# Two attentions on one core: local attention's channels loaded in quarters of 32 partitions, and a split made in place

## The chip, the cores and the metric

The kernel runs on one core of a Trainium2 chip. The metric is the device time of one execution in microseconds (us); the median of three runs is given. The core's engines run side by side: TensorE (PE for its matmuls, PEld for its weight loads), VectorE (DVE), ScalarE (ACT), GpSimd (POOL), and SyncE (SP), which here does nothing but issue DMAs. Each engine works through its own instructions in order and waits for semaphores.

## The reference, cut to what matters

```python
S, D, H, Dh, W, dil = 2048, 576, 32, 18, 8, 2
# A: local, dilated: each position sees itself and 7 positions 2, 4, ... 14 before it
q, k, v = heads(A_x @ A_wqkv)
idx = pos[:, None] - dil * arange(W)          # masked where negative
logits = einsum("bhsd,bhswd->bhsw", q, k[idx]) * Dh ** -0.5
a = merge(einsum("bhsw,bhswd->bhsd", softmax(logits), v[idx])) @ A_wo
# B: full attention of the same size
q, k, v = heads(B_x @ B_wqkv)
b = merge(softmax(q @ k.T * Dh ** -0.5) @ v) @ B_wo
return concatenate([a, b], -1)                # 1 x 2048 x 1152, float32
```

## The kernel before, in words

Matmuls take their operands as a rounded high part and a remainder, so most inputs are split in two on the way: ACT copies the high part (a copy that rounds), POOL or DVE subtracts it from the raw value.

*First phase, to about 422 us: the projections of A and B.* `inputs` (L387) splits the rows of x chunk by chunk. A is 576 = 4 x 128 + 64 rows deep; the last 64 rows of x are loaded twice into one tile of 128 partitions, so that their high part and their remainder lie in the two halves of one tile, `xhl` (L401): ACT copies the high part into one half (L404), copies the other half's high part into a helper tile `ohi` (L405), and POOL or DVE writes the other half's remainder from raw and helper (L406). The name `ohi` is a ring of four buffers. It is shared: the copies of projection results on their way to DRAM take from it too (L462 with its store at L468 into `dqk`, and L651 with its store at L652 into `da`). The transposed projections of A lie in DRAM as `da`, 3 x 576 rows (the channels of q, k, v) of 14 + 2048 positions; the 14 are the halo before the first position.

*Second phase, 422 to 1635 us: 512 steps* (`while step < ALL`, L1132). They are the 8 groups of 4 heads, 4 blocks of 512 queries each, 16 tiles of 128 keys each of B's full attention. A step makes four score matmuls (L229) with ACT's exponentials (L235), three or four matmuls whose results DVE reduces to the maxima that a later block needs (L159, L166), and the weighted sums of an earlier tile (L701). Sixteen steps are one block. After each block `finish` (L706) divides by the row sums: at one step after the block's end SP loads the 2048 sums into `den` (L733), at eight DVE takes the reciprocals (L734), at nine SP stores them, at thirteen SP loads them spread out as `rec` (L736), and at eighteen POOL multiplies (L737). Other things on SP are the `place` loads of maxima (L192, eight of 2 KB for a block), the stacks of later groups (L144), outputs, and the loads of A.

*A's local attention* is POOL's work beside the steps. It is cut into eight sub-blocks of 256 positions (`local(j)`, L815). A sub-block lies on 128 partitions: 4 quarters of 64 positions times 32 heads, with 18 channels x 64 positions (q) or 18 x 78 (k and v, with their halo) along each partition. The products with q and k are L841 to L848, those with v L884 to L887. Sub-block j has its origin at step 10 + 54 j.

What sets the order is written out by hand: each function appends pieces to `agenda` at a step, `due()` runs those of the current step, and each engine's instructions stand in the order in which they were issued so. A SP load therefore waits behind all SP loads issued before it. SP's DMAs use eight semaphores in turn, so each also waits until the one issued eight before it has landed.

Before the change a sub-block's data come in two hops. `arrange(n)` (L820), for n = q, k, v, copies from `da` to a DRAM tensor `dpart`, which holds the sub-block in the tile's order (4 quarters x 576 channels x 64 or 78 positions): one DMA each of 576, 702 and 702 KB, in runs of 256 or 312 bytes. The three are issued at consecutive steps, 24 steps ahead of the origin or at the fourteenth step of that block if that is later (j = 4: steps 206 to 208). `fetch(nm)` (L826) then loads `dpart` into the tile in one DMA over 128 partitions: q at the origin, k one step later, v 28 steps later. The tile of q has one buffer, k and v share two.

Of the kernel before, what the change touches and what calls it, by code (L numbers as in the profile page):

```python
# [7 lines left out]
F32 = mybir.dt.float32  # L8
F32R = mybir.dt.float32r
BF16 = mybir.dt.bfloat16  # L10
AF = mybir.ActivationFunctionType
# [5 lines left out]
S = 2048  # L17
D = 576
H = 32
DH = 18  # L20
# [9 lines left out]
NJ = S // AB  # L30
SUB = AB // 4
HALO = DIL * (W - 1)

STEPS = NB * NT
# [9 lines left out]
GAP = 54  # L44

A_FROM = 10


def ap(t, *dims):

    return bass.AP(tensor=t.tensor, offset=t.offset, ap=[list(t.ap[0])] + [list(d) for d in dims])


def rows(t, *dims):

    return bass.AP(tensor=t.tensor, offset=t.offset, ap=[list(d) for d in dims])
# [3 lines left out]
def two_attentions(ctx: ExitStack, tc, xa, wa, woa, xb, wb, wob, out):  # L60
# [5 lines left out]
    nc = tc.nc  # L66
    load = nc.sync.dma_start

    const = ctx.enter_context(tc.tile_pool(name="const", bufs=1))
    dram = ctx.enter_context(tc.tile_pool(name="dram", bufs=1, space=DRAM))  # L70
# [9 lines left out]
    def bank(kind=None):  # L80
# [6 lines left out]
    dqk = dram.tile([2, 2 * D, S], F32, name="dqk")  # L87
    dv = dram.tile([NG, 128, NT, 4 * 19], F32, name="dv")


    da = dram.tile([3 * D, HALO + S], F32, name="da")
    dparts = [[dram.tile([4, D, (HALO if n else 0) + SUB], F32, name=f"dpart{n}{j}") for n in range(3)]
              for j in range(NJ)]
    dao = dram.tile([NJ, 2, 4, D, SUB], F32, name="dao")
    drec = dram.tile([NG, NB, 4, 512], F32, name="drec")
    do = dram.tile([2, NG - 1, 128, S], F32, name="do")
# [242 lines left out]
    with (tc.tile_pool(name="x", bufs=1, side="right") as xp,  # L339
# [14 lines left out]
        def staged(src, cols, dims, into, spare=False):  # L354

            n = sum(m for _, m in cols)
            wide = src.shape[1]
            raws = {}

            def get(c, issue=load):  # L360
                t = raws[c] = raw(spare)
                for at, r0, m in [(0, 128 * c, 128)] if c < 4 else [(0, 512, 64), (64, 512, 64)]:
                    issue(ap(t[at : at + m], (n // len(cols), len(cols)), (1, n // len(cols))),  # L363
                          rows(src[r0, cols[0][0]], (wide, m), *dims))

            return get, lambda c: into(c, raws[c][:, :n])

        def split(engine, hi, lo, t):
            nc.scalar.activation(hi, t, AF.Copy)  # L369
            engine.tensor_sub(lo, t, hi)  # L370
# [19 lines left out]
        def inputs(src, b, engine, spare=False):  # L390
            x = [[], [], None]

            def into(c, t):
                if c < 4:
                    hi, lo = (xp.tile([128, 512], F32R, name=nm, bufs=4 * NB) for nm in ("xhi", "xlo"))
                    x[0].append(hi)
                    x[1].append(lo)
                    split(engine, hi, lo, t)
                else:

                    hl = x[2] = xp.tile([128, 512], F32R, name="xhl", bufs=NB)  # L401
                    high = xp.tile([128, 512], F32R, name="ohi", bufs=4)
                    one, other = (slice(64 * (b % 2), 64 * (b % 2) + 64), slice(64 - 64 * (b % 2), 128 - 64 * (b % 2)))
                    nc.scalar.activation(hl[one], t[one], AF.Copy)  # L404
                    nc.scalar.activation(high[other], t[other], AF.Copy)  # L405
                    engine.tensor_sub(hl[other], t[other], high[other])  # L406

            return x, *staged(src, [(512 * b, 512)], [(512, 1), (1, 512)], into, spare)

# [30 lines left out]
        qkv, odd = ExitStack(), ExitStack()  # L440
# [3 lines left out]
        if True:  # L444
# [34 lines left out]
            for c in range(5):  # L479
                one, other = (load, nc.scalar.dma_start) if c % 2 == 0 else (nc.scalar.dma_start, load)  # L480
# [159 lines left out]
            for k in range(2, 14):  # L640
                n = 46 if k == 2 else 36 + 4 * k
# [7 lines left out]
            def leave_a(c, b, n, ps):  # L649
                o = xp.tile([128, 512], F32, name="ohi", bufs=4)  # L650
                nc.scalar.activation(o[:n], ps, AF.Copy)  # L651
                load(da[128 * c : 128 * c + n, HALO + 512 * b : HALO + 512 * b + 512], o[:n])  # L652
# [23 lines left out]
            for c, b in order:  # L676
                n = min(128, 3 * D - 128 * c)
                work_list.append(((b % 2, ws[c][0], xas[b][0], slice(0, n), every),
                                  lambda ps, n=n: ps[:n], lambda ps, c=c, b=b, n=n: leave_a(c, b, n, ps)))
# [16 lines left out]
    work = ctx.enter_context(tc.tile_pool(name="work", bufs=1, reuse_waits="tile"))  # L696
# [118 lines left out]
    def local(j):  # L815

        st = {}
        p0 = AB * j

        def arrange(n):  # L820
            wide = (HALO if n else 0) + SUB
            load(rows(dparts[j][n][0, 0], (wide, D), (D * wide, 4), (1, wide)),
                 rows(da[D * n, HALO + p0 + SUB - wide :], (HALO + S, D), (SUB, 4), (1, wide)))


        def fetch(nm):  # L826
            halo = 0 if nm == "q" else HALO
            n = DH * (halo + SUB)
            t = st[nm] = work.tile([128, DH, halo + SUB], F32, name="akv" if halo else "aq", bufs=2 if halo else 1)
            load(ap(t, (1, n)), rows(dparts[j]["qkv".index(nm)][0, 0], (n, 128), (1, n)))  # L830

        def window(t, c):

# [46 lines left out]
        def weighted(c):  # L880
            if c == 0:
                st["o"] = work.tile([128, DH, SUB], F32, name="ao", bufs=1)
            at = wide()
            nc.gpsimd.tensor_mul(at, ap(st["lg"], (0, 2), (SUB, W), (1, SUB)), window(st["v"], c))  # L884
            nc.gpsimd.tensor_add(at[:, :, :4], at[:, :, :4], at[:, :, 4:])  # L885
            nc.gpsimd.tensor_add(at[:, :, :2], at[:, :, :2], at[:, :, 2:4])
            nc.gpsimd.tensor_add(st["o"][:, 2 * c : 2 * c + 2], at[:, :, 0], at[:, :, 1])  # L887
# [10 lines left out]
        def put(i):  # L898
            load(rows(dao[j, i, 0, 0], (DH * SUB, 128), (1, DH * SUB)),
                 ap(st["parts"][i].bitcast(F32), (1, DH * SUB)))  # L900
# [18 lines left out]
        def sums_of_a(h):  # L919
# [3 lines left out]
            if h == 0:  # L923
# [3 lines left out]
            nc.scalar.activation(y, two, AF.Copy)  # L927
            behind_scores.append(lambda: nc.vector.tensor_add(y, one, y))

        pieces = [(0, lambda: fetch("q")), (1, lambda: fetch("k")), (28, lambda: fetch("v")), (33, lower),  # L930
                  (35, exponents), (39, share), (60, upper), (61, rest), (64, lambda: put(0)), (66, lambda: put(1))]

        pieces[:0] = [(at, lambda f=f, n=n: f(n)) for f, ats in ((most, (31, 32, 33)), (total, (36, 37, 38)),
                                                                (inverses, (38, 39))) for n, at in enumerate(ats)]
        for c in range(DH // 2):
            pieces.append((5 + 5 * c // 2, lambda c=c: match(c)))
            pieces.append((39 + 5 * c // 2, lambda c=c: weighted(c)))
        at = A_FROM + GAP * j - 24

        at = max(at, STEPS * (at // STEPS) + 14) - A_FROM - GAP * j  # L940
        for n in range(3):
            pieces.append((at + n if j else n - 7, lambda n=n: arrange(n)))
        for n, (at, ends) in enumerate(((70, (78, 80)), (81, (87, 89)))):
            pieces.append((at, lambda n=n: get(n)))
            for h in range(2):
# [144 lines left out]
    for j in range(NJ):  # L1090
        plan(A_FROM + GAP * j, local(j))
# [15 lines left out]
    rest = NG * NB * PIECES * 2 - early  # L1107
# [24 lines left out]
    while step < ALL:  # L1132
        n, kt = divmod(step, NT)
# [51 lines left out]
```

## Time and profile before

| what | time |
|---|---|
| median of 3 runs | 1646.02 us (1645.42 to 1647.79) |
| the profiled execution | 1646.54 us |
| its span, first to last instruction | 1644.8 us |
| PE busy | 1633.1 us |
| DVE busy | 1397.0 us |
| ACT busy | 1221.9 us |
| POOL busy | 959.2 us |
| data moved by DMA | 188.22 MB, 114 GB/s on the mean |

The profile gives for each engine the time in which it worked; issuing DMAs is not counted as work, so SP has a queue but no busy share. PE's and PEld's times overlap. A row of a timeline gives the start, the duration, the engine and line, the operation, the tiles (out <- in) and the count; in brackets stands the idle time before it and what ended it. For a DMA on SP's queue the duration is the time that SP's sequencer stood on that instruction, waits included, not the transfer. The chain of work that ended last is followed back from the last instruction: a piece that isn't PE is a place at which PE waited for it. In a table of windows the last three columns are the granted clock of PE as a share of full speed, the share of time in which the 16 DMA engines were busy (packets of several queues overlap, so it can exceed 1), and the data rate.

### The profile page before, as it was taken

What the parts mean: (1) busy time and instruction counts of PE and PEld (TensorE: products, weight loads), DVE (VectorE), ACT (ScalarE), POOL (GpSimd) and SP (SyncE); (2) the same over time, 40 slices, a digit from 0 to 9 for tenths busy, and PEclk for the clock granted to TensorE, in tenths of its full rate; (3) what the DMA queues carried; (4) which work ended last, traced back from release to release, by engine and by line L of the source; (5) the groups of instructions that cost most, each with busy time, mean ns of one, the idle gap of its engine ahead of it and who ended that gap; (6) DMA issues with size and microseconds to landing.
All of it is one profiled execution on the core that took longest, in us unless ns stands there. A gap on an engine that the chain in (4) does not pass through costs nothing.

```text
span 1644.8 us, 33745 instructions
## 1 busy us (share of the span) xinstructions
PE 1633.1 (99%) x12906; PEld 935.0 (57%) x12906; DVE 1397.0 (85%) x2366; ACT 1221.9 (74%) x2419; POOL 959.2 (58%) x792
## 2 busy tenths in 40 slices
PE   9999999999999999999999999999999999999998
PEld 7999879998433444444344344344344344445676
DVE  5199989999899989889889899889899989888533
ACT  6314432111899998998998998998998998998554
POOL 2306642210195995994994994994995996940000
PEclk9999999999999999999999999999999999999999
DMA  8837955522515347157139325716526132033201
GB/s 252 238 113 204 257 165 140 134 87 90 95 48 100 98 120 135 54 139 143 53 93 161 82 77 130 147 65 122 134 79 117 65 107 78 21 114 123 101 37 59
DMA packets 188353, 188.22 MB, mean 114 GB/s; under 512 B 118384, under 2 KB 132208, under 8 KB 186464
## 3 DMA queue, kind: packets, MB, share of 16 engines
q1 hardware_dynamic: 183328, 174.53, 40.9%
q0 software_dynamic: 4032, 10.63, 3.0%
q8 instruction: 101, 1.65, 0.4%
q10 hardware_dynamic: 832, 0.92, 0.2%
q14 instruction: 60, 0.49, 0.1%
HBM read 113.16 MB, written 88.12 MB: 122 GB/s over the span
## 4 chain that ended last, share of the span: by engine, by line
PE 96%; DMA 2%; DVE 1%; ACT 0%; POOL 0%; issue 0%; SPq 0%; ACTq 0%; POOLq 0%; DVEq 0%
PE po L701 30%; PE bank L229 25%; PE bank L322 16%; PE bank L159 13%; PE bank L1010 7%; PE bank L259 5%; DMA den<-o 1%; DVE mx L166 1%; DMA dqk<-ohi 0%; POOL xlo L370 0%; DMA first<-xb 0%; DVE am L859 0%; SPq L363 0%; DMA out<-y 0%; PE bank L985 0%
## 5 line engine op out<-in xcount | busy, mean ns | idle before, releaser
L166 DVE TENSOR_REDUCE mx<-bank 128x1 f32<-128x512 f32 x2048 | 1288.1, 683 | 144.6 <-PE bank L159 115.8
L235 ACT ACTIVATE e<-bank 128x512 f32<-128x512 f32 x2048 | 1060.2, 613 | 94.3 <-PE bank L229 51.0
L159 PE MATMUL bank<-ks,qs 54*128 54x512 f32 x2048 | 752.7, 423 | 2.1 <-DVE mx L166 2.0
L229 PEld LDWEIGHTS bank<-qs,ks 56*128 56x128 f32 x2048 | 331.1, 186 | 454.1 <-ACT e L235 423.6
L229 PE MATMUL bank<-qs,ks 56*128 56x512 f32 x2048 | 582.0, 425 | 0.0
L701 PE MATMUL po<-e,v 128*19 128x512 f32 x4096 | 538.1, 599 | 0.0
L159 PEld LDWEIGHTS bank<-ks,qs 54*128 54x128 f32 x2048 | 340.8, 185 | 15.6 <-DVE mx L166 7.6
L841 POOL TENSOR_TENSOR pr<-aq,akv 128x1024 f32<-128x1024 f32 x72 | 158.4, 2201 | 28.1 <-DMA akv<-dpart 25.6
L701 PEld LDWEIGHTS po<-e,v 128*19 128x19 f32 x4096 | 70.6, 97 | 182.1 <-issue 171.4
L884 POOL TENSOR_TENSOR pr<-lg,akv 128x1024 f32<-128x1024 f32 x72 | 158.1, 2196 | 0.6
L845 POOL TENSOR_TENSOR pr<-pr 128x1024 f32<-128x1024 f32 x64 | 152.5, 2382 | 5.0
L651 ACT ACTIVATE ohi<-bank 128x512 f32<-128x512 f32 (+1 forms) x56 | 30.5, 595 | 148.3 <-issue 116.9
L322 PE MATMUL bank<-xlo,ahi 64*128 64x512 f32 (+1 forms) x448 | 117.9, 389 | 1.4 <-POOL xlo L370 1.4
L322 PE MATMUL bank<-xhi,alo 64*128 64x512 f32 (+1 forms) x448 | 116.1, 388 | 0.0
L322 PE MATMUL bank<-xhi,ahi 64*128 64x512 f32 (+1 forms) x448 | 113.7, 388 | 1.1 <-ACT ohi L651 1.1
L885 POOL TENSOR_TENSOR pr<-pr 128x512 f32<-128x512 f32 x72 | 92.3, 1282 | 5.6
L370 POOL TENSOR_TENSOR alo<-raw,ahi 128x512 fp32r<-128x512 f32 (+1 forms) x14 | 17.6, 1254 | 121.1 <-ACT ahi L369 86.7
L463 POOL TENSOR_TENSOR olo<-olo,ohi 128x512 fp32r<-128x512 f32 x36 | 46.1, 1294 | 63.8 <-ACT ohi L462 58.4
L737 POOL TENSOR_TENSOR o<-o,rec 128x512 f32<-128x512 f32 x29 | 37.2, 1284 | 64.3 <-DMA rec<-drec 35.4
L322 PEld LDWEIGHTS bank<-xlo,ahi 64*128 64x128 f32 (+1 forms) x448 | 67.2, 182 | 7.6 <-POOL xlo L370 2.5
L322 PEld LDWEIGHTS bank<-xhi,alo 64*128 64x128 f32 (+1 forms) x448 | 65.8, 182 | 5.3
L322 PEld LDWEIGHTS bank<-xhi,ahi 64*128 64x128 f32 (+1 forms) x448 | 63.8, 181 | 7.2 <-ACT ohi L651 1.5
(197 smaller groups left out, 1790.5 us busy)
## 6 DMA issues: line engine op xcount, KB each, us to landing
do<-n SPq DMA_DIRECT2D x28, 512.0 KB
da<-ohi SPq DMA_DIRECT2D x52, 256.0 KB
dpart<-da SPq DMA_DIRECT2D x16, 702.0 KB
akv<-dpart SPq DMA_DIRECT2D x16, 702.0 KB
out<-y SPq DMA_DIRECT2D x32, 288.0 KB
qs<-dqk SPq DMA_DIRECT2D x30, 288.0 KB
ks<-dqk SPq DMA_DIRECT2D x30, 288.0 KB
at<-dao SPq DMA_DIRECT2D x64, 128.0 KB
```

The costliest lines, as they stand in the source:

```text
L159: nc.tensor.matmul(ps, qs[at, b, p, 128 * t : 128 * t + 128], ks[at, p, 512 * k : 512 * k + 512], start=True, stop=True)
L166: nc.vector.tensor_reduce(mx[:, r, p, t, k : k + 1], ps, axis=AX.X, op=ALU.max)
L229: nc.tensor.matmul(ps, ks[at, p, 128 * kt : 128 * kt + 128], qs[at, b, p], start=True, stop=True)
L235: nc.scalar.activation(e, ps, AF.Exp, scale=SCALE)
L259: nc.tensor.matmul(ps, a, b, start=c == i == 0, stop=c == 4 and i == 1)
L322: nc.tensor.matmul(ps, a, b, start=start, stop=stop)
L701: nc.tensor.matmul(po[32 * i : 32 * i + 19], vs[g][:, kt, 19 * i : 19 * i + 19], es[i], start=kt == 0, stop=kt == NT - 1)
L841: nc.gpsimd.tensor_mul(pr, ap(st["q"][:, 2 * c], (SUB, 2), (0, W), (1, SUB)), window(st["k"], c))
L845: nc.gpsimd.tensor_add(st["pr"], st["pr"], pr)
L884: nc.gpsimd.tensor_mul(at, ap(st["lg"], (0, 2), (SUB, W), (1, SUB)), window(st["v"], c))
L885: nc.gpsimd.tensor_add(at[:, :, :4], at[:, :, :4], at[:, :, 4:])
L1010: nc.tensor.matmul(ps, a, b, start=start, stop=stop)
```

## The change

The DRAM tensors `dpart` and the function `arrange` are gone. `fetch(nm, s)` loads quarter s of q, k or v, 32 partitions, straight from the rows of `da`: 32 heads x 18 channels x 64 or 78 positions, 576 runs of 256 or 312 bytes, 144 or 175.5 KB. A sub-block has twelve such DMAs where it had three copies and three fetches. For j > 0 the quarters of q are issued at 18, 16, 14 and 12 steps before the origin, those of k at 10, 8, 6 and 4 before it, those of v at 16, 18, 20 and 22 after it; for j = 0 those of q and k at nine to two steps before it, one per step.

In `inputs`, the last rows' high part of the other half is copied straight into `xhl` and the remainder written over it by a subtraction in place. The helper tile from the ring `ohi` is not taken any more.

The instructions of PE, DVE, ACT and POOL are the same in number and in order; only SP's differ.

```diff
-    dparts = [[dram.tile([4, D, (HALO if n else 0) + SUB], F32, name=f"dpart{n}{j}") for n in range(3)]
-              for j in range(NJ)]
...
                     hl = x[2] = xp.tile([128, 512], F32R, name="xhl", bufs=NB)
-                    high = xp.tile([128, 512], F32R, name="ohi", bufs=4)
                     one, other = (slice(64 * (b % 2), 64 * (b % 2) + 64), slice(64 - 64 * (b % 2), 128 - 64 * (b % 2)))
                     nc.scalar.activation(hl[one], t[one], AF.Copy)
-                    nc.scalar.activation(high[other], t[other], AF.Copy)
-                    engine.tensor_sub(hl[other], t[other], high[other])
+                    nc.scalar.activation(hl[other], t[other], AF.Copy)
+                    engine.tensor_sub(hl[other], t[other], hl[other])
...
-        def arrange(n):
-            wide = (HALO if n else 0) + SUB
-            load(rows(dparts[j][n][0, 0], (wide, D), (D * wide, 4), (1, wide)),
-                 rows(da[D * n, HALO + p0 + SUB - wide :], (HALO + S, D), (SUB, 4), (1, wide)))
-
-        def fetch(nm):
+        def fetch(nm, s):
             halo = 0 if nm == "q" else HALO
-            n = DH * (halo + SUB)
-            t = st[nm] = work.tile([128, DH, halo + SUB], F32, name="akv" if halo else "aq", bufs=2 if halo else 1)
-            load(ap(t, (1, n)), rows(dparts[j]["qkv".index(nm)][0, 0], (n, 128), (1, n)))
+            if s == 0:
+                st[nm] = work.tile([128, DH, halo + SUB], F32, name="akv" if halo else "aq", bufs=2 if halo else 1)
+            load(st[nm][32 * s : 32 * s + 32],
+                 rows(da[D * "qkv".index(nm), HALO + p0 + SUB * s - halo :],
+                      (DH * (HALO + S), H), (HALO + S, DH), (1, halo + SUB)))
...
-        pieces = [(0, lambda: fetch("q")), (1, lambda: fetch("k")), (28, lambda: fetch("v")), (33, lower),
-                  (35, exponents), (39, share), (60, upper), (61, rest), (64, lambda: put(0)), (66, lambda: put(1))]
+        pieces = [(33, lower), (35, exponents), (39, share), (60, upper), (61, rest), (64, lambda: put(0)), (66, lambda: put(1))]
...
-        at = A_FROM + GAP * j - 24
-
-        at = max(at, STEPS * (at // STEPS) + 14) - A_FROM - GAP * j
-        for n in range(3):
-            pieces.append((at + n if j else n - 7, lambda n=n: arrange(n)))
+
+        for nm, at, apart in (("q", -18, 2), ("k", -10, 2)) if j else (("q", -9, 1), ("k", -5, 1)):
+            pieces += [(at + apart * i, lambda nm=nm, i=i: fetch(nm, i)) for i in range(4)]
+        pieces += [(16 + 2 * i, lambda i=i: fetch("v", i)) for i in range(4)]
```

## Prediction

> **What bounds the kernel now.** I read the page first (shares, then the chain that ended last), then the chain and the queues around its largest DMA piece, then the one ACT wait on the lines that the change edits.
>
> ```profile
> span 1644.8 us, 33745 instructions
> ...
> PE 1633.1 (99%) x12906; PEld 935.0 (57%) x12906; DVE 1397.0 (85%) x2366; ACT 1221.9 (74%) x2419; POOL 959.2 (58%) x792
> ...
> PE po L701 30%; PE bank L229 25%; PE bank L322 16%; PE bank L159 13%; PE bank L1010 7%; PE bank L259 5%; DMA den<-o 1%; DVE mx L166 1%; DMA dqk<-ohi 0%; POOL xlo L370 0%; DMA first<-xb 0%; DVE am L859 0%; SPq L363 0%; DMA out<-y 0%; PE bank L985 0%
> ```
>
> TensorE is busy for 1633.1 of 1644.8 us, so all that any change of loads can give back is 11.7 us of idle time, and whatever a lowered clock stretches. The change doesn't touch a matmul. It can pay only where the chain leaves PE, and there two entries are DMAs of the middle of the kernel: `den<-o` and `dqk<-ohi`. Both lie next to lines that the change edits.
>
> The first is one place. The chain between 880 and 920 us (start, us, what), then the queue of SP (the engine that issues the loads) and DVE in that time:
>
> ```profile
> 896.44 0.07 PE bank L159
> 896.50 13.46 DMA den<-o
> 909.96 0.02 issue
> 909.99 0.25 DVE den L734
> 910.24 0.56 DVE mx L166
> ```
>
> ```profile
> 883.59 12.82 SPq L822 DMA_DIRECT2D dpart<-da  x3
> 896.50 5.74 SPq L733 DMA_DIRECT2D den<-o  x1
> 902.34 1.81 SPq L948 DMA_DIRECT2D out<-y  x1
> ```
>
> ```profile
> 909.99 0.25 DVE L734 RECIPROCAL den<-den 128x16 f32<-128x16 f32 x1 [2.44 <-DMA den<-o]
> ```
>
> The three copies from `da` to `dpart` occupy SP for 12.8 us, the 8 KB load of the denominators is issued behind them, lands only at 909.96, and DVE stands at the reciprocal for 2.44 us. Behind that reciprocal in DVE's order are the maxima (L166), and they release the banks that PE writes next:
>
> ```profile
> 906.22 1.05 PE L701 MATMUL po<-e,v 128*19 128x512 f32 x8
> ...
> 908.35 1.05 PE L701 MATMUL po<-e,v 128*19 128x512 f32 x8
> 909.33 0.50 PE L229 MATMUL bank<-qs,ks 56*128 56x512 f32 x1
> 910.84 0.49 PE L159 MATMUL bank<-ks,qs 54*128 54x512 f32 x1 [1.01 <-DVE mx L166]
> ...
> 912.46 1.30 PE L701 MATMUL po<-e,v 128*19 128x512 f32 x8
> ...
> 915.70 1.45 PE L701 MATMUL po<-e,v 128*19 128x512 f32 x8
> ...
> 918.21 1.05 PE L701 MATMUL po<-e,v 128*19 128x512 f32 x8
> ...
> 920.32 1.05 PE L701 MATMUL po<-e,v 128*19 128x512 f32 x8
> ```
>
> Each L701 row is one step. Undisturbed steps take 2.13 and 2.11 us (906.22 to 908.35, 918.21 to 920.32); the three in between take 4.11, 3.24 and 2.51. So the place costs 2.00 + 1.13 + 0.40 = 3.5 us, not the 1.0 us of PE's idle time: the second and third excess are the clock. Windows (PE, PEld, DVE, ACT, POOL busy; then clock, DMA share, GB/s):
>
> ```profile
> 896.00:908.00 12.00, 12.00 (x83) 5.15 (x82) 10.75 (x19) 11.02 (x22) 9.96 (x8) 1.00 1.28 114
> 908.00:912.00 4.00, 2.99 (x17) 0.91 (x14) 2.01 (x5) 2.79 (x6) 3.80 (x4) 1.00 0.19 35
> 912.00:916.00 4.00, 4.00 (x21) 1.63 (x24) 3.21 (x6) 2.76 (x7) 3.77 (x5) 0.64 0.84 259
> ```
>
> At a granted clock of 0.64, four microseconds hold 1.4 us less work, which agrees with 1.13 + 0.40. The first row shows why den is late: DMA fully occupied, at only 114 GB/s.
>
> **The change, part by part.**
>
> *1. The copies da to dpart go.* 24 DMAs in all, three per sub-block of A, eight sub-blocks:
>
> ```profile
> L822 SPq DMA_DIRECT2D dpart<-da x24: 536/642/9247, 422.1 to 1255.1; - x24
> ...
> L830 SPq DMA_DIRECT2D akv<-dpart x16: 327/426/587, 443.0 to 1367.4; - x16
> L830 SPq DMA_DIRECT2D aq<-dpart x8: 346/470/554, 442.6 to 1296.0; - x8
> ```
>
> Of the 24 the median holds SP for 0.64 us and the longest for 9.2; only the set ahead of block 12's den (issued at steps 206 to 208, den at 209) put itself on the chain. It goes: DVE finds den there, PE doesn't wait, and the clock has no cause to fall. Gain 3.5 us; the lower bound is 2.0, if the dip of the clock has another cause and stays. Nothing there is late next: the reciprocal's store and reload (L735, L736) follow one and five steps after it, and POOL multiplies by it only ten steps after it.
>
> *2. The new loads.* 96 quarters take the place of 24 whole fetches. No row shows a quarter; the nearest are the loads of `at` from `dao` (128 KB in runs of 256 B, which is q's run length) and the stack loads, whose destination is 18 partitions:
>
> ```profile
> L909 SPq DMA_DIRECT2D at<-dao x64: 359/505/3226, 587.1 to 1490.1; - x64
> ```
>
> ```profile
> L144 SPq DMA_DIRECT2D qs<-dqk x30: 743/772/971, 554.5 to 1154.9; - x30
> ...
> DMA to landing us min/median/max: 4.9/8.0/11.2
> ```
>
> A quarter has 576 runs (144 KB for q, 175.5 KB for k and v), so I estimate 0.5 to 0.8 us of SP, between the two medians, and take 0.6, nearer to `at` by its run length. Twelve are 7.2 us per sub-block. Before, SP spent 3 × 0.64 + 3 × 0.44 = 3.2 us of issue at the least. So SP works 4 us more per sub-block; but spread over 40 steps of 2.1 us, two steps apart. A den that comes behind a quarter is 0.6 us later, and has eight steps, 16.9 us, until its reciprocal; it lands in 8 us or less by the L144 row. The cover would be gone only if SP stood still for some 9 us. Cost 0; gain none below that, since SP is on no path. Upper end of the cost: one stall as measured, 3.5 us, for each den that is held so long.
>
> The rows also say that the quarter loads move 1.9 MB per sub-block once, where copies and fetches moved it twice, and none of it DRAM to DRAM.
>
> [...]
>
> *3. Buffers of q, k and v.* Loads are now issued 18 to 4 steps ahead (q, k) and 12 to 6 steps sooner (v), into one buffer for q and two for k and v. A quarter can stand on SP until POOL has finished the previous sub-block's products, and den, the places of maxima and stack loads stand behind it. POOL's last products of sub-block 6, and the releaser of what follows:
>
> ```profile
> 1244.84 2.38 POOL L845 TENSOR_TENSOR pr<-pr 128x1024 f32<-128x1024 f32 x1
> 1247.30 1.29 POOL L848 TENSOR_TENSOR lg<-pr 128x512 f32<-128x512 f32 x1
> 1254.40 1.29 POOL L865 TENSOR_TENSOR lg<-lg,am 128x512 f32<-128x512 f32 x1 [5.81 <-DVE am L859]
> ```
>
> The reads of q and k end before 1247.3. The last `aq` row of L830 above, 1296.0, is step 388; step 370, where sub-block 7's q is now issued, is 18 steps of 2.1 us earlier, at 1258.2. So 11 us of slack, five steps; the wait costs nothing. If POOL were later by 11 us plus the 9 us that den has to spare, den would stall.
>
> *4. The last rows' high part in place.* The helper tile `ohi` (four buffers, shared with the stores' tiles) has one user fewer per projection chunk. Where ACT waited, in the wait list, and where PE waited:
>
> ```profile
> ACT ohi L405 <- DMA dqk<-ohi: 6.8, 1, 6.8
> ```
>
> ```profile
> 216.63 0.63 ACT L405 ACTIVATE ohi<-raw 64x512 fp32r<-64x512 f32 x1 [6.75 <-DMA dqk<-ohi]
> 217.28 0.63 ACT L369 ACTIVATE xhi<-more 128x512 fp32r<-128x512 f32 x1
> ...
> 222.95 1.08 ACT L651 ACTIVATE ohi<-bank 128x512 f32<-128x512 f32 x2 [1.28 <-DMA dqk<-ohi]
> ```
>
> ```profile
> 220.68 0.50 PE L322 MATMUL bank<-xhi,ahi 64*128 64x512 f32 x2 [1.10 <-ACT ohi L651]
> ...
> 225.95 0.50 PE L322 MATMUL bank<-xlo,ahi 64*128 64x512 f32 x2 [0.84 <-POOL xlo L370]
> ```
>
> ```profile
> 212.00:220.00 8.00, 7.57 (x66) 5.87 (x62) 7.24 (x12) 1.82 (x3) 4.50 (x6) 1.00 0.89 270
> 220.00:226.00 6.00, 3.97 (x27) 2.26 (x27) 3.57 (x6) 4.50 (x8) 3.89 (x5) 1.00 0.81 254
> ```
>
> PE loses 0.43 + 2.03 = 2.46 us between 212 and 226. ACT's copy at 216.63 waits for a store of `dqk` to leave the buffer, and the splits of the next x rows (L369) stand behind it in ACT's order. After the change that copy needs no such buffer. But the store is no earlier: the evacuations L651 take from the same four buffers, and the pair at 222.95 waits for a store itself, while DMA is at 0.81 to 0.89 and hardly quicker. So the gain is between 0.5 us (only the first gap shortens) and 2.5 us (all of it); I take 1.5, the middle, since neither end is nearer to a row: one of the two named gaps is ACT's, one follows the store. The arithmetic itself, a subtraction in place, has the same shape, so 0.
>
> *Sum.* -3.5 (den with its clock) + 0 (quarters, buffers) - 1.5 (projection) = -5.0 us. The profiled execution took 1646.54 us, 0.5 above the median 1646.02 of the runs shown; on the median that gives 1641.0.
>
> **Rivals.**
>
> *The clock is not the stall's doing.* Against it: windows of 10 us over the whole span show a clock under 0.98 in one place, this one. For it: from 220 to 226 PE is busy for 3.97 of 6 us, worse than the 2.99 of 4 around the den, and the clock stays at 1.00. Then den gives 2.0 and the sum is -3.5, 1642.5; with the projection at its low end -2.5, 1643.5, which a measurement can't tell from no change (0.2%, 3.3 us). [...]
>
> *DMA was never what made den late in other executions.* The collision at 896 is a matter of microseconds; if the stall is only in the profiled run, -1.5 and 1644.5. Against: the profiled run is 0.5 us above the median, not 3.5.
>
> *SP is held by POOL (the other side).* A quarter of q waits for the buffer that POOL still reads, den stands behind it, and each such den costs 3.5 us. Den directly follows or lies among q's or k's quarters at five sub-blocks (steps 49, 161, 209, 273, 321); three stalls cost 10.5, less the gains of 5.0: about 1651.5; two, 1648. Against it: five steps of slack at sub-block 6. It decides when POOL is some 20 us later than in this trace. [...]
>
> *DVE and POOL meet differently.* POOL's work of each sub-block may begin some tenths sooner or later; worth a microsecond or two of either sign.
>
> **How the numbers follow.** Forecast, den with clock and part of the projection (1639 to 1642.7): 0.60. Clock not returned, or the stall not repeated (1642.7 to 1649.3): 0.22. SP held, or the orders of DVE and POOL or of the stores worse by more than 3.3 us: 0.18. Range: the low end takes both terms at their best (-6.0) and the fourth rival's two microseconds, 1638; the high end reaches into the third, two stalls, 1649. The likeliest case alone is 1638 to 1643.
>
> **What would show it.** No `den<-o` in the chain, steps 208 to 216 of 2.1 us, clock 1.00 there: part 1 right. SP rows of quarters of 0.5 to 0.8 us, none of several microseconds: parts 2 and 3 right; a quarter with POOL as its releaser and a den late behind it: wrong. PE idle under 1.5 us between 212 and 226: part 4 right. The prediction is wrong if a new DMA stands in the chain between 422 and 1635 us, or if the stall at 909 moves to another den.

## The result, and the profile after

The changed kernel takes 1640.39 us (median of six executions, 1639.34 to 1641.1) against 1646.36 us for the kernel before beside it (six executions, 1644.97 to 1650.26): a ratio of 0.9961, 95% interval 0.9948 to 0.9974. It was measured again in the experiments, twelve executions against thirty: 1640.27 against 1644.67 us, ratio 0.9976 (0.9966 to 0.9985). So the gain is 4.4 to 6.0 us, and the prediction of 1641.0 us holds; why the kernel before isn't always equally slow comes out below, in part.

The page of the profiled execution after (1641.08 us), in the same three rows as before:

```profile
span 1639.3 us, 33789 instructions
...
PE 1629.1 (99%) x12906; PEld 952.7 (58%) x12906; DVE 1395.2 (85%) x2366; ACT 1221.8 (75%) x2419; POOL 959.4 (59%) x792
...
PE po L697 30%; PE bank L226 25%; PE bank L319 14%; PE bank L156 13%; PE bank L1001 7%; PE bank L256 5%; DMA raw<-xa 1%; POOL xlo L367 1%; DVE mx L163 1%; DMA dqk<-olo 0%; DMA dqk<-ohi 0%; PE bank L471 0%; DMA more<-xa 0%; DVE am L852 0%; DMA out<-y 0%
```

`den<-o` has left the chain. The place where it stood, on SP's queue and on DVE (lines are four lower after the change):

```profile
889.43 0.59 SPq L729 DMA_DIRECT2D den<-o  x1
890.07 1.27 SPq L821 DMA_DIRECT2D aq<-da  x2
891.44 0.57 SPq L939 DMA_DIRECT2D out<-y  x1
```

```profile
905.86 0.24 DVE L730 RECIPROCAL den<-den 128x16 f32<-128x16 f32 x1
```

The den load takes 0.59 us of SP where it took 5.74, and no idle time stands at the reciprocal. The 32 and 64 quarter loads on SP (minimum, median, maximum in ns):

```profile
L821 SPq DMA_DIRECT2D akv<-da x64: 551/599/1752, 423.4 to 1340.6; - x64
L821 SPq DMA_DIRECT2D aq<-da x32: 562/614/826, 420.7 to 1264.4; - x32
```

The windows of the projection after, with the columns of the prediction's windows:

```profile
212.00:220.00 8.00, 8.00 (x72) 6.77 (x70) 7.24 (x12) 2.91 (x6) 6.92 (x8) 1.00 0.88 249
220.00:226.00 6.00, 5.90 (x51) 4.67 (x49) 5.42 (x10) 2.86 (x5) 4.59 (x4) 1.00 0.57 175
```

PE's idle time of 2.46 us between 212 and 226 is down to 0.10. But 20 us earlier a new one stands, 2.08 us, behind ACT's wait for a store of the remainders:

```profile
194.78 0.50 PE L319 MATMUL bank<-xhi,whi 64*128 64x512 f32 x2 [2.08 <-ACT olo L457]
```

```profile
194.13 0.60 ACT L457 ACTIVATE olo<-bank 128x512 f32<-128x512 f32 x1 [3.31 <-DMA dqk<-olo]
```

To divide the gain over the kernel, one row of each profile is enough: ACT's copies of the block results, 31 of them, with the start of the first and of the last. Before and after:

```profile
L710 ACT ACTIVATE o<-po x31: 597/633/636, 455.6 to 1570.7; 128x512 f32<-128x512 f32 x31
```

```profile
L706 ACT ACTIVATE o<-po x31: 598/632/637, 454.1 to 1564.8; 128x512 f32<-128x512 f32 x31
```

Up to the first copy the gain is 1.5 us, from the first to the last (1115.1 and 1110.7 us) 4.4, and behind the last -0.4. Block n is here the time from the n-th of these copies to the next. Of the 4.4, the starts of successive copies put 4.2 at block 13 (38.29 us before, 34.06 after), 0.4 at block 16, 0.3 at block 23, and take 0.6 back at block 9.

### The profile page after: what moved, and what is told of

It reads as the page before. It is cut to its first block, busy times and chain, and to the rows that moved or that the text cites. A ratio compares the mean times of both kernels' runs of the same rounds, so it can differ in the third digit from the quotient of the medians.

```text
span 1639.3 us, 33789 instructions
## 1 busy us (share of the span) xinstructions
PE 1629.1 (99%) x12906; PEld 952.7 (58%) x12906; DVE 1395.2 (85%) x2366; ACT 1221.8 (75%) x2419; POOL 959.4 (59%) x792
## 4 chain that ended last, share of the span: by engine, by line
PE 95%; DMA 2%; DVE 1%; POOL 1%; issue 0%; ACT 0%; SPq 0%; POOLq 0%; ACTq 0%; DVEq 0%
PE po L697 30%; PE bank L226 25%; PE bank L319 14%; PE bank L156 13%; PE bank L1001 7%; PE bank L256 5%; DMA raw<-xa 1%; POOL xlo L367 1%; DVE mx L163 1%; DMA dqk<-olo 0%; DMA dqk<-ohi 0%; PE bank L471 0%; DMA more<-xa 0%; DVE am L852 0%; DMA out<-y 0%
## 5 line engine op out<-in xcount | busy, mean ns | idle before, releaser
L319 PE MATMUL bank<-xlo,ahi 64*128 64x512 f32 (+1 forms) x448 | 113.1, 388 | 0.1
## 6 DMA issues: line engine op xcount, KB each, us to landing
akv<-da SPq DMA_DIRECT2D x64, 175.5 KB
```

Source lines behind the costliest of these rows:

```text
L319: nc.tensor.matmul(ps, a, b, start=start, stop=stop)
```

## The experiments

Theory: the change has two independent effects. The loads free block 12's den from the copies ahead of it (second phase), the split in place frees ACT from a buffer of the ring `ohi` (first phase). Rivals: one effect, in that a shift in time alone lets den miss the copies; the copies' traffic rather than their place in SP's queue; a gain of another chip.

### The two halves, each alone

The first drops the split in place from the changed kernel:

```diff
+                    high = xp.tile([128, 512], F32R, name="ohi", bufs=4)
...
-                    nc.scalar.activation(hl[other], t[other], AF.Copy)
-                    engine.tensor_sub(hl[other], t[other], hl[other])
+                    nc.scalar.activation(high[other], t[other], AF.Copy)
+                    engine.tensor_sub(hl[other], t[other], high[other])
```

The second makes the reverse edit in the kernel before, and keeps its copies.

> The quarter loads alone, with the helper tile for the last rows' high part kept. Theory (two independent terms, den's stall and the projection): the four microseconds at blocks 12 and 13 go, the projection stays as in the kernel before: 4.2 us under it (about 1642), with the 6.75 us wait of ACT for a store of dqk still there and 2.5 us of PE idle between 212 and 226. Rival (the new loads are worth nothing, or the gain came from the projection's shift in time, which let den miss the copies): within 1 us of the kernel before.

> The split in place alone, with the copies to dpart kept. Theory: 1.4 us under the kernel before (about 1645), PE idle of 2 us near 193 in place of the idle between 212 and 226, and den's stall of about 13 us on the chain in block 13 unchanged. Rival (a shift of 1.5 us at the start is enough for den to miss the copies): 5 us under it.

Measured: 1643.04 us (ratio 0.999, 0.9981 to 0.9999) and 1643.2 us (0.9994, 0.9986 to 1.0002) beside 1643.69 us of the kernel before, whose 35 executions here run from 1640.2 to 1648.9. Both gains, 0.65 and 0.5 us, are smaller than expected, the second can't be told from none, and the kernel before was 2.7 us quicker than in the prediction's result. In the profile of the first ACT still waits at 217 us (4.40 us), but PE stands for 0.08 us between 212 and 226, not for 2.5. The profile of the second shows why den's stall was worth less there. Its copies and den load on SP stand as in the kernel before, but den is later by less:

```profile
880.41 12.89 SPq L821 DMA_DIRECT2D dpart<-da  x3
893.40 5.69 SPq L732 DMA_DIRECT2D den<-o  x1
```

```profile
905.91 0.25 DVE L733 RECIPROCAL den<-den 128x16 f32<-128x16 f32 x1 [1.17 <-DMA den<-o]
```

DVE waits for 1.17 us, not 2.44; PE doesn't stand, the clock stays at 1.00, and block 13 takes 35.56 us, of which 0.8 has another cause (a sum on DVE, below). So den's lateness varies between executions around the point from which it costs anything. All four were therefore run once more, the changed kernel among them, on one chip.

> The changed kernel itself, beside its two halves on one chip, since the kernel before ran 2.7 us quicker on the chip of the first experiments than on that of the prediction's result. Theory (den's lateness behind the copies differs from run to run, from no wait to 2.4 us of DVE waiting and a lowered clock behind it): 2 to 5 us under the kernel before, and its times less spread than that one's. Rival (chip and place set the six microseconds): within 1 us of the kernel before.

> Quarter loads alone, again. Theory (the loads govern the second phase alone): from the first block's end to the last 1110 us, as in the changed kernel (1110.7), and 1 to 2.5 us behind the changed kernel in all, lost before 460 us. Rival (the two halves of the change are one effect): no slower than the changed kernel.

> The split in place alone, again. Theory (it governs the first phase alone): the first block ends at 452.5 to 454.5 us, as in the changed kernel, and from there to the last block's end it takes 1111 to 1115 us, as copies and fetches do; 1 to 4 us behind the changed kernel. Rival (one effect): no slower than the changed kernel.

Measured, beside 1644.67 us of the kernel before (1641.6 to 1647.8):

| kernel | median us | ratio (95%) | under the kernel before |
|---|---|---|---|
| both (the changed kernel) | 1640.27 | 0.9976 (0.9966 to 0.9985) | 4.4 |
| quarter loads alone | 1642.18 | 0.9985 (0.9975 to 0.9994) | 2.5 |
| split in place alone | 1642.60 | 0.9990 (0.9981 to 0.9999) | 2.1 |

In this set the halves add up, 2.5 + 2.1 = 4.6 against 4.4, with intervals of about 1.5 us to either side. In the first set they came to 1.1 us, while a kernel that differs from the changed one only by a fifth buffer (below) was 4.0 us under the kernel before there; what made the halves worth less on that chip stays open. The rows of ACT's block copies, for the loads alone and for the split alone, put each into its phase:

```profile
L707 ACT ACTIVATE o<-po x31: 597/630/632, 455.7 to 1565.4; 128x512 f32<-128x512 f32 x31
```

```profile
L709 ACT ACTIVATE o<-po x31: 597/630/632, 453.0 to 1565.9; 128x512 f32<-128x512 f32 x31
```

With the helper tile the first copy comes at 455.7 and with the split in place at 453.0; from first to last it takes 1109.7 us with quarter loads and 1112.9 with copies. Over all profiles of this study that don't stall on purpose, the five with the helper tile have their first copy at 455.2 to 457.5 and the eight with the split in place at 452.2 to 454.1 us: the ranges don't meet. The three that have the copies at their old place take 1112.5, 1112.9 and 1115.1 us from first to last; the seven with quarter loads and no copies 1109.6 to 1111.1. So the rival of one single effect falls; and as the four kernels ran on one chip here, the 4.4 us aren't a chip's.

In the split alone, den's wait was again another:

```profile
906.59 0.25 DVE L733 RECIPROCAL den<-den 128x16 f32<-128x16 f32 x1 [1.52 <-DMA den<-o]
```

Block 13 took 36.08 us there: 38.29, 35.56 and 36.08 are three executions with the copies, of which the prediction had seen the worst. In the kernel before, SP stood on den for 7.0 us at 636 and for 5.3 us at 1259 too, and DVE waited at no reciprocal but the one at 910: elsewhere den's cover was enough.

### The order on SP

The kernel before, with one set of copies behind block 12's den:

```diff
-        at = max(at, STEPS * (at // STEPS) + 14) - A_FROM - GAP * j
+        at = max(at, STEPS * (at // STEPS) + 14) - A_FROM - GAP * j + (6 if j == 4 else 0)
```

> The kernel before with the three copies of the fifth sub-block six steps later (212 to 214 in place of 206 to 208), so that block 12's den goes ahead of them. Theory (den stands behind the copies, the order on SP is the cause): 3.5 to 4.2 us under the kernel before, clock 1.00 everywhere. Rival (the copies' traffic itself, 2 MB from DRAM to DRAM, slows whatever lies beside it): the stall moves to drec and rec of the same block, or stays; within 1 us of the kernel before.

Measured: 1642.75 us, ratio 0.9991 (0.9981 to 1.0) beside 1643.69 us. The mechanism was as expected; den is issued ahead of the copies and DVE doesn't wait for it:

```profile
892.25 0.59 SPq L733 DMA_DIRECT2D den<-o  x1
892.89 0.59 SPq L822 DMA_DIRECT2D dpart<-da  x1
```

```profile
909.50 0.24 DVE L734 RECIPROCAL den<-den 128x16 f32<-128x16 f32 x1
```

Block 13 took 34.90 us. The size, 0.9 us at the median, is less than expected; that fits a kernel beside it that seldom has the full stall, but no profile of those executions shows it. What is left over 34.06 has another cause, in this run's rows of DVE and POOL:

```profile
895.97 1.13 DVE L859 TENSOR_TENSOR as<-as 128x64 f32<-128x64 f32 x1
```

```profile
895.73 1.29 POOL L737 TENSOR_TENSOR o<-o,rec 128x512 f32<-128x512 f32 x1 [7.37 <-ACT e L235]
```

A sum over 64 columns that takes 0.22 us in the changed kernel took 1.13: it began 0.24 us into POOL's multiplication by `rec` and ended 0.08 us after it. In the fourteen profiles this small sum takes 0.80 to 1.17 us where POOL still has 0.7 us or more of that multiplication to do (five profiles, the kernel before with 1.01 among them) and 0.21 to 0.29 in the nine others; in two of these it begins in the multiplication's last 0.1 or 0.2 us. So where the two meet, DVE's sum ended only behind POOL's operation, by 0.08 us in these rows and in the kernel before; by what means isn't shown. Whether they meet is a matter of a microsecond, and it costs block 13 some 0.5 to 0.9 us, an estimate from the sum's excess over 0.22 us and from the 34.58 and 34.90 us of the two among the five in which den was in time, against 34.06.

The meeting goes with the form of the loads. The five profiles are those of the five kernels that load A through `dpart`. Before and after:

```profile
882.95 0.58 SPq L736 DMA_DIRECT2D rec<-drec  x1
893.72 1.29 POOL L737 TENSOR_TENSOR o<-o,rec 128x512 f32<-128x512 f32 x1 [7.29 <-DMA rec<-drec]
894.08 1.01 DVE L859 TENSOR_TENSOR as<-as 128x64 f32<-128x64 f32 x1
```

```profile
880.34 0.58 SPq L732 DMA_DIRECT2D rec<-drec  x1
891.98 1.28 POOL L733 TENSOR_TENSOR o<-o,rec 128x512 f32<-128x512 f32 x1 [6.46 <-ACT e L232]
893.17 0.22 DVE L852 TENSOR_TENSOR as<-as 128x64 f32<-128x64 f32 x1
```

Counted from the start of block 13, `rec` is issued 6.5 to 7.1 us earlier in the five and 8.1 to 8.9 earlier with quarter loads, and POOL's multiplication starts 3.8 to 4.2 us after it in the five and 2.1 to 3.3 with quarter loads (the kernel with added stalls of DVE, below, left aside). The three copies aren't the cause: with them six steps later, as here, `rec` is as late as before, and with three put back into the changed kernel (next) it is issued 8.1 us ahead. What holds it on SP isn't shown. Block 16 has the same meeting at A's first maximum, `am<-lg`: 1.04 to 1.53 us in the five in place of 0.42, and the block takes 38.96 to 39.41 us there and 38.69 to 38.82 with quarter loads. In block 9 it is the other way round; the changed kernel:

```profile
749.63 1.29 POOL L733 TENSOR_TENSOR o<-o,rec 128x512 f32<-128x512 f32 x1 [3.33 <-DMA rec<-drec]
750.10 1.10 DVE L852 TENSOR_TENSOR am<-lg 128x256 f32<-128x256 f32 x1
```

Of the six profiles with quarter loads, split in place and no added stalls, five have this `am<-lg` at 0.76 to 1.51 us, beside POOL's work on a block's results, and block 9 at 40.55 to 41.31 us; the sixth and all profiles without both halves have 0.41 to 0.51 and 40.3.

The reverse, the copies put back into the changed kernel, where nothing uses them:

```diff
+        if j == 4:
+            pieces += [(n - 20, lambda n=n: arrange(n)) for n in range(3)]
```

> The changed kernel with three copies from da into an unused DRAM tensor put back at steps 206 to 208 (576, 702 and 702 KB), as the fifth sub-block had them. Theory (copies ahead of den on SP make it late): DVE waits 1 to 2.5 us for den again, block 13 takes 35.5 to 38.3 us in place of 34.1, 1.5 to 4 us behind the changed kernel. Rival (it was the traffic of all 24 copies, or the fetches): block 13 stays at 34.1.

Measured: 1640.82 us, ratio 0.9987 (0.9976 to 0.9997) beside 1643.65 us. The wait came back, at a price under the expected one (the kernel with bunched loads, below, took 1639.79 in this set):

```profile
880.83 13.50 SPq L820 DMA_DIRECT2D dpart<-da  x3
894.42 6.07 SPq L827 DMA_DIRECT2D aq<-da  x1
900.59 1.26 SPq L730 DMA_DIRECT2D den<-o  x1
```

```profile
906.78 0.25 DVE L731 RECIPROCAL den<-den 128x16 f32<-128x16 f32 x1 [1.29 <-DMA den<-o]
```

Block 13 takes 34.94 us, 0.9 more than without the copies and less than the 35.5 expected at the least. Three copies at this place are thus enough to make den late (a quarter of q between them and den stood for 6.07 us, where a quarter takes 0.6), and a wait of 1.3 us costs 0.9, since the sum on DVE took only 0.29 here; the other 21 copies aren't needed for it. With the sum's excess over 0.22 us taken off block 13's excess over 34.06, den's waits of 1.17, 1.52 and 2.44 us in the three kernels with the copies come to about 0.7, 1.1 and 3.4 us, an estimate from these rows; only the last has a lowered clock in it. An earlier wait of SP, of the kind of the prediction's rival on the other side, wasn't tried.

Is it SP's standing still, or the DMA engines behind it? One den load was issued by ACT in the kernel before:

```diff
-        for at, f in ((1, lambda: load(den, o[DH:128:32])),
+        for at, f in ((1, lambda: (nc.scalar.dma_start if (g, b) == (3, 0) else load)(den, o[DH:128:32])),
```

> The kernel before with the one den load of block 12 issued by ACT, not SP, all copies in place. If den's lateness is the time that SP stands on the copies, den is issued some 7 us sooner and lands in time: no wait of DVE, block 13 at 34 to 35 us, 1 to 3.5 us under the kernel before. If it is the queues of the DMA engines, full of the copies' runs, den lands as late as before and block 13 stays at 35.5 to 38.3 us.

Measured: 1642.9 us, ratio 0.9997 (0.9987 to 1.0007), no difference. In its profile den lands in time and block 13 takes 34.58 us (the sum on DVE took 0.80), but the copies moved as well:

```profile
884.54 0.58 SPq L736 DMA_DIRECT2D rec<-drec  x1
895.05 5.31 SPq L822 DMA_DIRECT2D dpart<-da  x3
```

The first copy was issued 9.9 us behind the end of `rec`, at 895.05, and ACT had issued den at 892.50; what the copy waited for isn't shown. So den went ahead of the copies here too, and the run doesn't tell the two apart. It stays open what SP stands on in those 12.8 us; the second of the three copies alone took 9.25 us in the kernel before, with no wait for a semaphore on its instruction in the trace, and the same three, six steps later, took 0.57 to 0.59 us each.

### The clock behind a wait

Extra reductions on DVE in the changed kernel, whose result nothing uses:

```diff
+        for _ in range({100: 1, 180: 2, 260: 3, 340: 4}.get(step, 0)):
+            nc.vector.tensor_reduce(idle[:54], sets[g % 3][1][:54, 0], axis=AX.X, op=ALU.max)
```

> The changed kernel with extra reductions on DVE, some 2.1 us each, that nothing uses: one at step 100, two at 180, three at 260, four at 340. PE should stand for about 1, 3, 5 and 7 us. If a short wait brings the clock down (as 1.0 us seemed to in block 13), the granted clock falls behind each. [...] If the dip in block 13 had nothing to do with the wait, behind none.

One execution was made (1666.55 us, with the stalls). PE's idle time in the rows behind the first two, and windows around the first, the second (two) and the third:

```profile
644.14 0.49 PE L156 MATMUL bank<-ks,qs 54*128 54x512 f32 x1 [0.73 <-DVE mx L163]
```

```profile
827.81 0.63 PE L156 MATMUL bank<-ks,qs 54*128 54x512 f32 x1 [2.90 <-DVE mx L163]
```

```profile
642.00:646.00 4.00, 3.27 (x19) 1.16 (x23) 4.00 (x6) 3.07 (x6) 0.00 (x0) 1.00 0.16 61
824.00:828.00 4.00, 1.10 (x10) 0.37 (x3) 3.97 (x4) 1.51 (x3) 4.00 (x4) 1.00 0.22 92
828.00:834.00 6.00, 6.00 (x25) 2.44 (x28) 4.09 (x8) 3.03 (x6) 5.92 (x3) 0.50 0.33 135
...
1021.00:1025.00 4.00, 3.52 (x21) 3.33 (x23) 2.82 (x5) 1.20 (x2) 0.00 (x0) 0.50 0.66 134
```

PE stood for 0.73, 2.90, 5.01 and 7.51 us. The clock stayed at 1.00 behind the first and fell to 0.50 behind (or within) the three others; after 2.90 us of waiting PE worked for 6 us at a clock of 0.50, which by these two numbers alone costs 3, an estimate. The kernel with the copies six steps later had a dip as well, in the projections, behind a wait for a buffer of `ohi`:

```profile
222.78 0.50 PE L322 MATMUL bank<-xhi,ahi 64*128 64x512 f32 x2 [2.83 <-ACT ohi L651]
```

```profile
225.00:228.00 3.00, 3.00 (x16) 2.08 (x16) 1.38 (x2) 1.51 (x3) 3.00 (x3) 0.50 0.88 263
```

So in this case a dip went with each long wait: in the fourteen profiles the four waits of PE of 2.83 us and more (2.83, 2.90, 5.01 and 7.51) all had one, at a clock of 0.50. Of the twelve between 0.6 and 2.1 us behind PE's start, eleven had none (2.10 us the longest); the twelfth is the 1.01 us in block 13 of the kernel before. That its dip was the stall's doing is therefore argued, not shown: it is the longest of the den waits, and no profile without such a wait has a dip there, but it is one execution.

### Two sizes: the next buffer, and the form of the loads

Five buffers of the remainders' tile in the changed kernel, measured in both sets:

```diff
-                lo = low.tile([128, 512], F32R, name="olo", bufs=4)
+                lo = low.tile([128, 512], F32R, name="olo", bufs=5)
```

> The changed kernel with five buffers in place of four for the remainders' tile olo. Theory (the change freed ACT of one wait, for a buffer of ohi, and met the next, for a buffer of olo, at 194 us, which costs PE 2.1 us): that idle time goes, 1.5 to 2 us under the changed kernel (about 7.5 under the kernel before). Rival (SP's order is what ends last there, with loads of x behind stores in its queue): no change from the changed kernel.

> The changed kernel with five buffers of olo, again, now beside the changed kernel. Theory (the buffer of olo was the next wait of the projections): 1 to 2 us under the changed kernel, first block's end at 452.5. Rival (the first phase differs by as much from run to run): equal to the changed kernel within its interval.

Measured: 1639.74 us in the first set (ratio 0.9978, 0.9969 to 0.9987), 1639.99 in the second (0.9973, 0.9962 to 0.9984), there beside 1640.27 of the changed kernel: no difference that can be told. The reading was wrong. In the repeated profile of the changed kernel the idle time near 193 isn't there with four buffers either, as its row shows:

```profile
190.00:196.00 6.00, 6.00 (x56) 4.91 (x54) 5.92 (x10) 2.68 (x6) 4.65 (x5) 1.00 1.08 253
```

and the first copy came at 452.2. The projections' DMA arrives a little differently each time, with DMA engines at a share of 1.08 in that window, and the 2.08 us are likely such a chance: in the fourteen profiles such idle times, 0.7 to 2.1 us, stand near 174 in five and near 194 in two, with and without the helper tile. (Block 13 took 34.94 us in the second profile with five buffers: there the sum over 128 columns met POOL's multiplication, 1.33 us in place of 0.28.)

The quarters of q, k and v issued four at a time, and those of v spread over every fourth partition, so that A's sums read v of other positions than they should:

```diff
-            load(st[nm][32 * s : 32 * s + 32],
+            load(st[nm][s:128:4] if nm == "v" else st[nm][32 * s : 32 * s + 32],
...
-        for nm, at, apart in (("q", -18, 2), ("k", -10, 2)) if j else (("q", -9, 1), ("k", -5, 1)):
+        for nm, at, apart in (("q", -18, 0), ("k", -10, 0)) if j else (("q", -9, 1), ("k", -5, 1)):
...
-        pieces += [(16 + 2 * i, lambda i=i: fetch("v", i)) for i in range(4)]
+        pieces += [(16, lambda i=i: fetch("v", i)) for i in range(4)]
```

> The changed kernel with the four quarters of q, of k and of v each issued at one step; those of v go to every fourth partition and not to 32 neighbouring ones, so A's output is not the reference's. By the steps of the prediction both edits cost nothing (loads are off the path): within 1 us of the changed kernel. [...]

Measured: 1639.79 us, ratio 0.9977 (0.9967 to 0.9987), as the changed kernel (0.9976 in its set). Neither spacing nor rate is on the path. Two windows with nothing but small DMAs beside the quarters, the first of v (spread, sub-block 0), the second of k (32 neighbours, sub-block 1):

```profile
474.00:476.00 2.00, 2.00 (x16) 0.78 (x15) 1.77 (x4) 1.95 (x5) 1.92 (x2) 1.00 1.03 243
526.00:528.00 2.00, 2.00 (x19) 0.81 (x15) 1.62 (x4) 1.96 (x5) 1.92 (x2) 1.00 1.19 198
```

In these two windows the same runs move at 243 GB/s into spread partitions and at 198 into neighbours, 0.81 of it; the cause isn't shown. Four quarters are on their way together in both windows, so the rate of one quarter alone isn't measured by them.

## Why the prediction was right

*What bounds, and den's stall.* Right as to place and mechanism: `den<-o` left the chain, the steps of block 13 have their 2.1 us, and the copies put back bring the wait back. The term of 3.5 us is the size of one execution, and there the changed profile confirms it: block 13 gave 4.2 us, of which the DVE sum beside POOL's multiplication was 0.8. But it isn't the mean. In two other profiles with the copies, DVE's wait was 1.2 and 1.5 us where the prediction read 2.4, the clock kept, and den cost about 0.7 and 1.1. The loads alone were worth 2.5 us at the median of one set and 0.65 in the other. The rival that den is late only in some executions was thus partly true, and its argument against itself, that the profiled run lies 0.5 us above the median, didn't tell: executions of the kernel before lay 8.7 us apart (1640.2 to 1648.9), more than any den wait read here cost (0.7 to 3.4 us).

*The clock.* The prediction counted 1.5 us of dip with the stall. In that execution the dip is there, and its steps add up with it; that a wait of PE of 1.0 us brings it isn't borne out by the others. Behind 2.83 and 2.90 us of PE idle time the clock fell to 0.50; of the twelve waits between 0.6 and 2.1 us eleven had no dip. A fall behind 1.01 us, once, is left without a cause that a run shows.

*The quarters.* Estimated 0.6 us of SP each, measured 0.599 and 0.614 at the median, 1.75 at the most. Cost 0 is right: four at once made no difference. The cover that the prediction named (den has eight steps) was never used, as no den took SP longer than 0.63 us. In the two windows with four quarters at once, 32 neighbouring partitions took 198 GB/s and spread ones 243, a fifth less for the neighbours; no run shows the rate of a quarter alone, and none why the two differ.

*Buffers of q, k and v.* Right: no quarter stood on SP for POOL's products (0.5 us, behind a `mt`, is the longest wait of a quarter for POOL), so the rival on the other side had no part in it. It counted five sub-blocks whose quarters lie about a den; step 113, between k's third and last quarter, is a sixth, and its den too was issued in 0.59 us.

*The projection.* Predicted 1.5, in the profiled pair 1.5, at the median 2.1 for the split alone in one set and 0.5 in the other, and 3 between the means of the first copies' starts (456.3 and 453.1 us). The mechanism is right: ACT waits 4.4 to 6.75 us before the split near 217 us in all five profiles with the helper tile, in four of them for a store of `dqk`, and in none of the nine others. The two limits, 0.5 and 2.5, were drawn around one spot from 212 to 226 us. There PE stands for 0.08 to 3.07 us in the five and for 0.10 in the nine, and once the clock fell behind it; the rest of the 3 us lies elsewhere in the phase. The step "the store is no earlier, so part of the wait stays" failed in its place: the idle time went from 2.46 to 0.10 us there, and what was left of it stood 20 us earlier in that one execution.

*What the sum lacked.* The meetings of DVE and POOL. The prediction had them as a rival of either sign and put them at nothing in the sum; they go with the loads and have both signs: 0.5 to 0.9 us gained in block 13, 0.4 in block 16, and 0.6 lost in block 9 of the profiled pair, as in four of the five other profiles with both halves. Block 23's 0.3 us is less sure: three kernels with the copies take 36.6 to 36.9 us there and the changed one 36.3, but the two others that load through `dpart` take 36.3 and 36.4. So that the sum came out at 5.0 us is in part luck: den's term is too large for most executions seen, the projection's rather too small, and gains that the sum didn't count fill what is missing.

## What to carry to other kernels

A queue that works in order made a small load late behind the large ones before it (den was issued behind 12.8 us of copies and held SP for 5.74 us itself, 0.59 without them): look at what stands ahead of an 8 KB load with a due time before looking at bandwidth. A term read from one stall of one execution has the size of that execution; where the stall is a matter of a microsecond of slack, its size in others can be a third or less (about 0.7 and 1.1 us here, against 3.4). A change of loads also shifted when other engines began, and so which of their instructions met (one DVE sum of block 13 took 1.01 us before and 0.22 after): compare the durations of the same instruction in both profiles. When two edits touch different phases, a row that is common to all profiles, such as the first and last result copy, separates them better than the total time does.

## What was not expected of the hardware

The granted clock fell to 0.50 behind 2.90 us of PE idle time and stayed there for 6 us of full work, so a wait of DVE that stops PE for 3 us cost 6 to 7 (block 11 took 40.85 us with it and 34.22 without). The kernel before varied over 9 us between executions (1640.2 to 1648.9, 35 of them), the changed one over 1.8 us in six and, but for one execution of 1646.8, 4.2 in twelve. A DVE sum of 0.22 us that starts beside a POOL operation ended only behind it and took up to 1.17 us. An issue of a copy between two DRAM tensors in runs of 312 bytes held SP for 9.25 us with no semaphore to wait for.
